# Half-width first pass for four token blocks instead of two in an attention and two-MLP kernel

## The chip, the cores and the metric

One core of a Trainium2 chip runs the whole program in one launch. The metric is the device time of one execution in microseconds (us). Below, TensorE is PE, its weight loads PEld, VectorE DVE, ScalarE ACT, GpSimd POOL, and SP the engine that only issues transfers.

## The reference

Banded attention with 32 global tokens (batch 4, 8 heads, 544 positions, head dimension 64), then a squared-ReLU MLP, then a gated linear MLP. All arrays are fp32.

```
s_g = scale * q_g @ k_all.T ;           out_g = softmax(s_g) @ v_all
s_l = concat(scale * q_l @ k_g.T, banded(scale * q_l @ k_l.T))
out_l = softmax(s_l) @ v_all
x = concat(out_g, out_l) as (2176 tokens, 512)
x = (relu(x @ w_in) ** 2) @ w_out        # first MLP: 512 -> 2048 -> 512
y = ((x @ w1) * (x @ w2)) @ w3 @ w_out2  # second MLP
```

## The kernel before, in words

**Precision.** Every fp32 factor of a large product is split into a high and a low part, and a product is three matmuls (`PASSES`, line 66): high times high, high times low, low times high. So each weight has to be brought to that form first. `conv(n)` (line 527) does it for one piece of 128x512: two ACT instructions (lines 441, 444), two DVE instructions (452, 457), one POOL addition (523 or 513), and a split on ACT (465) and DVE (466).

**Blocks and halves.** The 2176 tokens are 8 blocks of 256 or 288 tokens, two to a batch. The first MLP is cut in two halves of its 2048 hidden columns. In its first half a block needs 16 converted pieces: 8 of `w_in` (0 to 7) and 8 of `w_out` (8 to 15). `h_unit` (line 579) computes 128 hidden columns of a block with 12 matmuls, then ReLU and square on ACT and the split of the result; `x_chain` (line 601) sums 128 of the 512 output columns over the hidden ones. Its result, a partial sum, goes to DRAM (`part_d`) and is added to the second half's later.

**Few blocks.** The first blocks come before all 16 pieces are converted. `width(i)` (line 81) says how many of a block's 8 hidden units are passed the first time: `HEAD` = 4 for the blocks below `FEW` = 2, 8 for the others. What the first two blocks leave out is done behind block 7, by `rows` (line 625) with the pieces 4 to 7 and 12 to 15, and `end_few` (line 724) adds it to the partial sum that `load_x` (line 715) has read back.

**Order.** The outer loop (line 730) goes over pairs of blocks. In the pair i the MLP of blocks i and i+1 is the main list of steps; the attention of the next batch (`cycle`, line 377: scores `sc` and `sg`, softmax on DVE and ACT, transposes `tp` and `tg`, the product `o` with the values) is laid between its steps by `merge` (line 643), and so are the conversions, the pieces 8 to 15 within the first pair. The first block of a pair needs the attention that was laid between the pair before: the copies of `o` to `xb` on ACT, their cast `hl` (line 571) and their split on DVE. From block 6 on there is no attention left. Behind the blocks' rest follow the first MLP's second half and the second MLP.

What stands in the program's text is not yet the order of an engine: the framework orders every engine's instructions anew, by readiness and a planned time, except where `keep_in_program_order` ties two. Each engine then works strictly in that order. The PSUM tiles `sc`, `tp`, `tg` and `o` share four banks (tag `at`).

Of the kernel before, what the change touches and what calls it, by code (L numbers as in the profile page):

```python
# [60 lines left out]
def block(i):  # L61
    i %= NBLK
    return S * (i // 2) + HALF * (i % 2), HALF if i % 2 == 0 else S - HALF
# [9 lines left out]

HEAD, FEW = 4, 2
ORDERED = (0, 1, 2, 3, 8, 9, 10, 11, 4, 5, 6, 7, 12, 13, 14, 15)
BREAKS = (*RUNS, 2 * HEAD)

# [1 line left out]
def width(i):  # L81
    return HEAD if i < FEW else 8
# [33 lines left out]
def attention_mlp(ctx: ExitStack, tc: tile.TileContext, kq0, kq, vw, wts, mask, ident, out_d):  # L116
# [321 lines left out]
    def conv_a(n):  # L438
        raw = raw_t.pop(n)
        t = [pools["cv"].tile([128, 512], I32, tag=f"wt{k}", name="wt", bufs=2) for k in range(3)]  # L440
        first = nc.scalar.activation(t[0].bitcast(F32), raw[:, :, 1].bitcast(F32), AF.Copy, scale=2.0**-112)
        if n >= 2 * HEAD:
            tc.keep_in_program_order(first)
        nc.scalar.activation(t[2], raw[:, :, 0].bitcast(U32), AF.Copy, scale=2.0**-29)
        mid_t[n] = t
        ahead = n + (4 if n < RUNS[1] else 3)
        if ahead < RUNS[1] or RUNS[1] <= n and ahead < RUNS[2]:
            load_w(ahead)

    def conv_b(n):  # L450
        a, b, _ = mid_t[n]
        first = nc.vector.tensor_scalar(
            out=b, in0=a, scalar1=3, scalar2=0x7FFFFFF8, op0=ALU.logical_shift_left, op1=ALU.bitwise_and
        )
        if n >= 2 * HEAD:
            tc.keep_in_program_order(first)
        nc.vector.scalar_tensor_tensor(  # L457
            out=b, in0=a, scalar=-(1 << 31), in1=b, op0=ALU.bitwise_and, op1=ALU.bitwise_or
        )
# [43 lines left out]
    def conv_c(n):  # L503
        _, b, m = mid_t.pop(n)
        if n >= PAIRED:
            k, u = divmod(n - PAIRED, 2)
            if u == 0:
                both_t[k] = unit("u1", F32)
                if "s" in both_t:
                    o, x, s = both_t.pop("s")  # L510
                    nc.sync.dma_start(out=both_d[o], in_=x)
                    nc.sync.dma_start(out=sums_d[o], in_=s)
            nc.gpsimd.tensor_tensor(out=both_t[k][:, u].bitcast(I32), in0=b, in1=m, op=ALU.add)  # L513
            if u == 1:
                x = both_t.pop(k)
                s = add_up(x, "u1", nc.vector)
                if k < 4:
                    both_t["s"] = k, x, s
                else:
                    for f in split_blocks(FIRST[k - 4], k, x, s, "u1"):  # L520
                        f()
            return
        nc.gpsimd.tensor_tensor(out=b, in0=b, in1=m, op=ALU.add)  # L523
        t = w_t[ORDERED[n] if n < RUNS[1] else n] = unit(UNITS[n])
        split_w(t, slice(0, 512), b.bitcast(F32))

    def conv(n):

        if n in BREAKS:
            conv_a(n)  # L530
        else:
            conv_c(n - 1)
        conv_b(n)
        if n + 1 in BREAKS:
            conv_c(n)
        else:
            conv_a(n + 1)
# [22 lines left out]
    def x_parts(i, k, n):  # L560

        t = xb_t[i, k] = fixed[4 * (i % 2) + k] if fixed else parts(NB)
        return t[:, :, :n]

    def of_split(i, k):
        s, n = block(i)
        return xs_d[:, k, :, s : s + n]
# [7 lines left out]
    def load_split(i, k, turn=1):  # L575
        t = xh[NBLK * turn + i, k] = x_parts(i, k, block(i)[1])
        nc.sync.dma_start(out=t.bitcast(F32), in_=of_split(i, k))

    def h_unit(i, f, w):
        n = block(i)[1]  # L580
        h = ps.tile([128, 512], F32, tag="h", name="h", bufs=H_BUFS)[:, :n]
        w = w_t[w]
        chain(h, [(w[:, a, 128 * k : 128 * (k + 1)], xh[i, k][:, b]) for k in range(4) for a, b in PASSES])
        r = sb.tile([128, NB], F32, tag="tmp", name="r", bufs=4)[:, :n]
        g = g_t[f] = fixed[8 + f % 6][:, :, :n] if fixed else parts(n)
        nc.scalar.activation(r, h, AF.Relu)  # L586
        nc.scalar.activation(g[:, 0], r, AF.Square)  # L587
        if i < SHARED:
            nc.vector.tensor_tensor(out=r, in0=r, in1=r, op=ALU.mult)
        else:  # L590
            nc.scalar.activation(r, r, AF.Square)  # L591
        split_lo(nc.vector, g[:, 1], r, g[:, 0])
# [3 lines left out]
    def staged(i, d):  # L596
        if d == 0:
            st_t[0] = sb.tile([128, 4, NB], F32, tag="st", name="st", bufs=1)[:, :, : block(i)[1]]
        return st_t[0][:, d, :]
# [25 lines left out]
    def rows(i, w_in, w_out, split, end, at=0):  # L625

        n, m = block(i)[1], len(w_in)
        steps = []
        for f in range(m + 1):
            if f < m:  # L630
                steps.append(lambda f=f: (h_unit(i, f, w_in[f]), store_now() if f == 1 else None))
            if at <= f < at + 4:
                steps.append(lambda f=f: split(f - at))
            if f > 0:
                steps.append(lambda f=f: x_add(i, f - 1, w_t[w_out[f - 1]], n, f == m))
        steps.append(lambda: [end(d) for d in range(4)])
        return steps

    def of(t, i):
        s, n = block(i)  # L640
        return t[:, :, s : s + n]
# [53 lines left out]
    main = [lambda f=f: h_unit(0, f, f) for f in range(width(0))]  # L695
# [9 lines left out]
    def split_a(i, d):  # L705
        if i < NBLK:
            split_x(i, d, xcols(i)[:, d])
        else:
            load_split(0, d, 2)
# [5 lines left out]
    def load_x(i):  # L715

        if i < NBLK:
            if "x" not in extra:
                extra["x"] = sb.tile([128, 4, 2 * NB], F32, tag="xb", name="xl", bufs=2)
            at = NB * (i % 2)  # L720
            t = x_t[i] = extra["x"][..., at : at + block(i)[1]]
            nc.sync.dma_start(out=t, in_=of(part_d, i))

    def end_few(i, d):
        nc.vector.tensor_tensor(out=staged(i, d), in0=acc[d], in1=x_t[i][:, d], op=ALU.add)
        if d == 3:
            nc.sync.dma_start(out=of(part_d, i), in_=st_t[0])
            load_x(i)

    for i in range(0, NBLK, 2):  # L730
        main = []
        for j in (i, i + 1):
            if j >= SHARED:
                if j == SHARED:
                    main.append(fix_places)
                main += rows(
                    j, range(8), range(8, 16),
                    lambda d, j=j: split_a(j + 1, d), lambda d, j=j: end_a(j, d, acc[d]),
                )
                continue  # L740
            if j > 0:
                main += [lambda f=f, j=j: h_unit(j, f, f) for f in range(width(j))]
            main += [lambda d=d, j=j: x_unit_a(j, d) for d in range(4)]
        b = i // 2 + 1
        if b < B:
            if b == 1:
                load_kq(H // 2)
                for k in range(H, H + 4):
                    load_v(k)
            steps = [s for j in range(4 * b - 1, 4 * b + 4) for s in cycle(j, j < 4 * b + 3, j >= 4 * b)]  # L750
            fills = [(steps, 0, len(main) - 5)]
            if b == 1:
                fills.append(([lambda n=n: conv(n) for n in range(2 * HEAD, 16)], 0, len(main)))
        else:
            for cm in (at_cm, rot_cm, cv_cm):
                cm.__exit__(None, None, None)
            pools["u2"] = ctx.enter_context(pool("u2", "right"))
            cv_cm = pool("cv2")
            pools["cv"] = cv_cm.__enter__()
            extra["w"] = sb.tile([128, 8 * NB], F32, tag="xb", name="wx", bufs=2)  # L760
            for k in range(16, 19):
                load_w(k)
            main.insert(18, lambda: (load_x(0), load_x(1)))
            for j in range(FEW):
                main += rows(
                    2 * NBLK + j, range(HEAD, 8), range(8 + HEAD, 16),
                    (lambda d: load_split(1, d, 2)) if j == 0 else lambda d: load_split(0, d),
                    lambda d, j=j: end_few(j, d),
                )
            fills = [([lambda n=n: conv(n) for n in range(16, 30)], 0, len(main))]  # L770
        merge(main, *fills)
# [187 lines left out]
    main = []  # L959
    for i in range(NBLK):  # L960
# [3 lines left out]
            lambda d, i=i: end_b(i, d), 0 if i < NBLK - 1 else 4,  # L964
# [102 lines left out]
    main = []  # L1067
# [140 lines left out]
```

## Time and profile before

| what | value |
| --- | --- |
| median of 3 runs | 861.88 us (860.67 to 863.28) |
| the profiled execution | 860.88 us, its span 859.1 us |
| busy: PE, PEld | 826.6 us (96%), 789.1 us (92%) |
| busy: DVE, ACT, POOL | 588.9 us (69%), 493.6 us (57%), 222.2 us (26%) |
| mean granted PE clock over the span | 0.99 |

The span is what lies between the first and the last instruction; the time of an execution is 1.78 us more. A row of the timeline is one or more like instructions in a run: its start in us from the span's start, its duration, engine, line, operation, what it writes and reads, how many, and in brackets the idle time before it with what ended it. The matmuls of a run overlap each other; the distance between the starts of two runs is therefore the better price for the first of them. A row of the stretches gives for each engine the busy time and the instructions in it, then the granted PE clock as a share of full speed.

### The profile page before, as it was taken

What the parts mean: (1) busy time and instruction counts of PE and PEld (TensorE: products, weight loads), DVE (VectorE), ACT (ScalarE), POOL (GpSimd) and SP (SyncE); (2) the same over time, 40 slices, a digit from 0 to 9 for tenths busy, and PEclk for the clock granted to TensorE, in tenths of its full rate; (3) what the DMA queues carried; (4) which work ended last, traced back from release to release, by engine and by line L of the source; (5) the groups of instructions that cost most, each with busy time, mean ns of one, the idle gap of its engine ahead of it and who ended that gap; (6) DMA issues with size and microseconds to landing.
All of it is one profiled execution on the core that took longest, in us unless ns stands there. A gap on an engine that the chain in (4) does not pass through costs nothing. (4 is left out here: it accounts for less than half of the span.)

```text
span 859.1 us, 17937 instructions
## 1 busy us (share of the span) xinstructions
PE 826.6 (96%) x6664; PEld 789.1 (92%) x6664; DVE 588.9 (69%) x1617; ACT 493.6 (57%) x1325; POOL 222.2 (26%) x264
## 2 busy tenths in 40 slices
PE   5789889999999999999999999999999999989998
PEld 4568779999999999999999999999999999989998
DVE  7878979773856576676742027796885857689862
ACT  7767977663767787777763246777311211355650
POOL 3401322000200333233330003330287445442000
PEclk9899989999999999999999999999999999999999
DMA  9935442333050776775853239745347544839931
GB/s 330 276 126 160 150 128 64 108 108 123 27 178 26 255 252 204 267 234 172 255 165 120 68 119 329 250 159 173 126 157 251 164 143 137 288 127 323 337 142 53
DMA packets 89879, 151.96 MB, mean 177 GB/s; under 512 B 6336, under 2 KB 63296, under 8 KB 89792
## 3 DMA queue, kind: packets, MB, share of 16 engines
q1 hardware_dynamic: 89792, 150.82, 53.4%
q8 instruction: 52, 0.85, 0.4%
q14 instruction: 35, 0.29, 0.1%
HBM read 103.42 MB, written 47.38 MB: 176 GB/s over the span
## 5 line engine op out<-in xcount | busy, mean ns | idle before, releaser
L162 PE MATMUL h<-hl,u 128*128 128x256 f32 (+1 forms) x1536 | 229.4, 291 | 6.1 <-ACT hl L571 4.9
L162 PEld LDWEIGHTS h<-hl,u 128*128 128x128 f32 x1536 | 205.1, 188 | 12.3 <-ACT hl L571 5.8
L816 PE MATMUL m<-hl,u 128*128 128x272 f32 x1296 | 171.2, 288 | 2.8 <-DVE r L838 1.5
L816 PEld LDWEIGHTS m<-hl,u 128*128 128x128 f32 x1296 | 165.5, 188 | 3.4 <-DVE r L838 2.0
L620 PE MATMUL acc<-hl,u 128*128 128x256 f32 (+1 forms) x1056 | 153.2, 288 | 0.2 <-DVE hl L151 0.2
L620 PEld LDWEIGHTS acc<-hl,u 128*128 128x128 f32 x1056 | 141.1, 188 | 1.2 <-DVE hl L151 0.4
L151 DVE TENSOR_TENSOR hl<-r,hl 128x288 fp32r<-128x288 f32 (+1 forms) x128 | 75.8, 598 | 76.1 <-ACT r L591 75.2
L523 POOL TENSOR_TENSOR wt<-wt 128x512 int32<-128x512 int32 x56 | 73.8, 1318 | 205.6 <-DVE wt L457 130.8
L586 ACT ACTIVATE r<-h 128x288 f32<-128x288 f32 (+1 forms) x128 | 49.7, 393 | 70.6 <-PE h L162 70.0
L162 PE MATMUL x<-hl,u 128*128 128x256 f32 (+1 forms) x480 | 70.4, 294 | 0.6 <-ACT pg L294 0.6
L816 PE MATMUL m<-u,u 128*128 128x272 f32 x528 | 70.3, 286 | 0.4 <-DVE r L836 0.2
L237 ACT ACTIVATE p<-p,st 128x192 f32<-128x192 f32 (+1 forms) x128 | 58.9, 464 | 16.0 <-DVE st L233 15.9
L816 PEld LDWEIGHTS m<-u,u 128*128 128x128 f32 x528 | 67.2, 188 | 0.8 <-DVE r L836 0.4
L162 PEld LDWEIGHTS x<-hl,u 128*128 128x128 f32 x480 | 62.9, 188 | 3.3 <-ACT pg L294 1.4
L466 DVE TENSOR_TENSOR u<-wt,u 128x512 fp32r<-128x512 f32 x56 | 40.3, 720 | 35.3 <-ACT u L465 34.7
L833 ACT COPY r<-m 128x272 f32<-128x272 f32 x40 | 15.4, 384 | 75.2 <-PE m L816 70.3
L270 POOL CAST qgp<-kq_hl 64x32 fp32r<-64x32 f32 x48 | 22.7, 473 | 138.5 <-PE sg L162 102.9
L1010 POOL TENSOR_TENSOR rs<-rs 128x272 f32<-128x272 f32 x64 | 56.2, 888 | 3.4
L587 ACT ACTIVATE hl<-r 128x288 fp32r<-128x288 f32 (+1 forms) x128 | 54.4, 432 | 4.0 <-ACT r L586 1.2
L1009 POOL TENSOR_TENSOR rs<-rs 128x272 f32<-128x272 f32 x32 | 28.2, 880 | 103.2 <-DVE rs L846 103.2
L457 DVE SCALAR_TENSOR_TENSOR wt<-wt 128x512 int32<-128x512 int32 x72 | 49.5, 688 | 1.6
L513 POOL TENSOR_TENSOR u<-wt 128x512 int32<-128x512 int32 x16 | 22.5, 1411 | 102.9 <-DVE wt L457 81.9
(113 smaller groups left out, 1309.4 us busy)
## 6 DMA issues: line engine op xcount, KB each, us to landing
wraw<-in_wts SPq DMA_DIRECT2D x37, 512.0 KB, 4.4
q_d<-rs SPq DMA_DIRECT2D x16, 952.0 KB, 5.3
rl<-q_d SPq DMA_DIRECT2D x12, 1088.0 KB, 7.3
wx<-in_wts SPq DMA_DIRECT2D x19, 512.0 KB, 5.1
u<-in_wts SPq DMA_DIRECT2D x16, 512.0 KB, 6.3
v_f<-in_vw SPq DMA_DIRECT2D x24, 256.0 KB, 2.9
hl<-xs_d SPq DMA_DIRECT2D x20, 288.0 KB, 4.1
hl<-xs_d SPq DMA_DIRECT2D x20, 256.0 KB, 4.4
```

Source lines behind the costliest of these rows:

```text
L151: eng.tensor_tensor(out=lo, in0=raw, in1=hi.bitcast(F32), op=ALU.subtract)
L162: mm(o, w, x, start=(k == 0), stop=(k == len(terms) - 1))
L237: nc.scalar.activation(p[:, c], p[:, c], AF.Exp, bias=least[:, n : n + 1], scale=-1.0, accum_out=sums[:, n, 0:1],)
L457: nc.vector.scalar_tensor_tensor(out=b, in0=a, scalar=-(1 << 31), in1=b, op0=ALU.bitwise_and, op1=ALU.bitwise_or)
L466: s = nc.vector.tensor_tensor(out=t[:, 1, cols], in0=raw, in1=t[:, 0, cols].bitcast(F32), op=ALU.subtract)
L523: nc.gpsimd.tensor_tensor(out=b, in0=b, in1=m, op=ALU.add)
L586: nc.scalar.activation(r, h, AF.Relu)
L587: nc.scalar.activation(g[:, 0], r, AF.Square)
L620: mm(acc[d], w[:, a, 128 * d : 128 * (d + 1)], g_t[f][:, b], start=(f + k == 0), stop=(last and k == 2),)
L816: mm(o, w, x, start=(i in (1, 6, 5, 4) and k == 0), stop=(k == len(terms) - 1), skip_group_check=(i in (2, 7, 3)),)
L1009: nc.gpsimd.tensor_tensor(out=u.c12, in0=u.c12, in1=u.c22, op=ALU.mult)
L1010: sub = lambda o, a, c: nc.gpsimd.tensor_tensor(out=o, in0=a, in1=c, op=ALU.subtract)
```

## The change

`FEW` becomes 4: blocks 2 and 3, too, pass only 4 of 8 hidden units the first time, and their rest is made behind block 7 with that of blocks 0 and 1. The conversions of the pieces 8 to 11 stay with the first pair's list, those of 12 to 15 go to the second pair's. The loads of the split inputs and of the partial sums for the four rests go round by block.

```diff
-HEAD, FEW = 4, 2
+HEAD, FEW = 4, 4
...
     def end_few(i, d):
         if d == 3:
             nc.sync.dma_start(out=of(part_d, i), in_=st_t[0])
-            load_x(i)
+            load_x((i + 2) % FEW)
...
-            if b == 1:
-                fills.append(([lambda n=n: conv(n) for n in range(2 * HEAD, 16)], 0, len(main)))
+            if b < 3:
+                some = ((2 * HEAD, 12), (12, 16))[b - 1]
+                fills.append(([lambda n=n: conv(n) for n in range(*some)], 0, len(main)))
...
             for j in range(FEW):
                 main += rows(
                     2 * NBLK + j, range(HEAD, 8), range(8 + HEAD, 16),
-                    (lambda d: load_split(1, d, 2)) if j == 0 else lambda d: load_split(0, d),
+                    lambda d, j=j: load_split(j + 1, d, 2) if j + 1 < FEW else load_split(0, d),
                     lambda d, j=j: end_few(j, d),
                 )
```

How the engines' order answers to it is seen at two places. The first is DVE at the end of the first pair, where the last two of the 16 conversions stand (L452 and L457 are the conversion's first two instructions on DVE, L466 its last; `u_...` is the converted piece; L151 splits the first block of the second pair). A row with - is of before, with + of the change:

```order
 L452 TENSOR_SCALAR wt<-wt 128x512
 L457 SCALAR_TENSOR_TENSOR wt<-wt 128x512
 L354 COPY xb<-o 128x32
 L151 TENSOR_TENSOR hl<-xb,hl 128x256
-L466 TENSOR_TENSOR u_1795<-wt,u_1795 128x512
-L452 TENSOR_SCALAR wt<-wt 128x512
+L466 TENSOR_TENSOR u_2676<-wt,u_2676 128x512
 L288 TENSOR_REDUCE stg_91<-sg 64x1
+L452 TENSOR_SCALAR wt<-wt 128x512
 L356 TENSOR_TENSOR xb<-xb,o 128x32
 L288 TENSOR_REDUCE stg_91<-sg 64x1
```

The names differ, and one conversion instruction has moved behind one other row. All rows of DVE ahead of these are the same in both, the conversions among them.

The second place is PE in the second pair, where the last heads of the second batch get their scores (`sc`) and the softmax of the heads before is transposed (`tp`, from `p_...`); `h` and `x` are the MLP's matmuls. Before:

```order
L162 MATMUL h<-hl,u_1128 128x288 x3
L156 MATMUL sc<-kq_hl 128x192
L162 MATMUL h<-hl,u_1128 128x288 x3
L156 MATMUL sc<-kq_hl 128x192 x5
L156 MATMUL sc<-kq_hl 128x224 x6
L320 MATMUL tp<-ident_sb,p_82 128x128 x4
L320 MATMUL tp<-ident_sb,p_83 128x128 x4
L162 MATMUL h<-hl,u_1128 128x288 x6
L162 MATMUL h<-hl,u_1373 128x288 x12
L307 MATMUL tg<-ident_sb,pg 128x64 x5
L156 MATMUL sc<-kq_hl 128x224 x6
L156 MATMUL sc<-kq_hl 128x192 x6
```

The same place in the change:

```order
L162 MATMUL h<-hl,u_222 128x256
L162 MATMUL h<-hl,u_293 128x256
L320 MATMUL tp<-ident_sb,p_80 128x128 x4
L162 MATMUL h<-hl,u_222 128x256 x2
L162 MATMUL h<-hl,u_293 128x256 x2
L320 MATMUL tp<-ident_sb,p_81 128x128 x4
L156 MATMUL sc<-kq_hl 128x192 x6
L156 MATMUL sc<-kq_hl 128x224 x6
L320 MATMUL tp<-ident_sb,p_82 128x128 x4
L320 MATMUL tp<-ident_sb,p_83 128x128 x4
L307 MATMUL tg<-ident_sb,pg 128x64 x5
L156 MATMUL sc<-kq_hl 128x224 x6
```

Before, 18 `h` matmuls of block 3 stand between `tp` and `tg`, and 63 of its `x` matmuls follow behind the last `o` of the batch. In the change block 3's matmuls are used up ahead of these rows; the `h` matmuls left are the first unit's of block 4, which wait for this very attention.

## Rows read from the trace of the kernel before

**Rows 1.** The page, busy time of each engine: us, share, instructions.

```profile
PE 826.6 (96%) x6664; PEld 789.1 (92%) x6664; DVE 588.9 (69%) x1617; ACT 493.6 (57%) x1325; POOL 222.2 (26%) x264
```

**Rows 2.** Stretches: length, busy PE PEld DVE ACT POOL, PEclk, DMA share, GB/s.

```profile
88.00:107.00 19.00, 16.74 (x176) 14.58 (x173) 18.91 (x77) 18.14 (x60) 6.84 (x10) 1.00 0.51 157
...
115.00:131.00 16.00, 12.29 (x110) 10.17 (x107) 11.95 (x38) 11.51 (x33) 2.79 (x2) 0.79 0.40 123
...
140.00:500.00 360.00, 360.00 (x2914) 343.49 (x2913) 214.75 (x604) 234.62 (x612) 67.14 (x65) 1.00 0.49 156
...
340.00:370.00 30.00, 30.00 (x244) 30.00 (x243) 22.02 (x42) 24.15 (x56) 7.80 (x6) 1.00 0.77 259
```

**Rows 3.** Timeline of PE, the end of the first pair and the second's start.

```profile
100.95 2.30 PE L156 MATMUL o<-pt_f,v_f 128*64 128x160 f32 x36
...
113.13 0.77 PE L162 MATMUL x<-hl,u 128*128 128x288 f32 x4
113.74 0.64 PE L162 MATMUL h<-hl,u 128*128 128x256 f32 x4
114.31 0.34 PE L307 MATMUL tg<-ident_sb,pg 64*128 64x64 f32 x2
...
115.47 2.60 PE L156 MATMUL o<-pt_f,v_f 128*64 128x160 f32 x36
118.89 1.09 PE L320 MATMUL tp<-ident_sb,p 128*128 128x128 f32 x8 [0.82 <-DVE p L245]
121.46 1.21 PE L162 MATMUL h<-hl,u 128*128 128x256 f32 x6 [1.48 <-ACT hl L571]
123.99 1.94 PE L320 MATMUL tp<-ident_sb,p 128*128 128x128 f32 x8 [1.32 <-DVE p L245]
125.86 4.25 PE L156 MATMUL o<-pt_f,v_f 128*64 128x160 f32 x36
130.04 1.02 PE L162 MATMUL sg<-kq_hl,qgp 128*128 128x288 f32 x6
...
131.27 0.97 PE L162 MATMUL h<-hl,u 128*128 128x256 f32 x6
```

**Rows 4.** Timeline of DVE between the same rows.

```profile
116.03 0.38 DVE L233 CUSTOM_DVE_ANT_0 p<-sc,mask_sb 128x224 f32<-128x224 f32 x1
...
117.92 0.68 DVE L466 TENSOR_TENSOR u<-wt,u 128x512 fp32r<-128x512 f32 x1
118.53 0.56 DVE L245 TENSOR_SCALAR p<-p,st 128x192 f32<-128x192 f32 x2
119.00 0.42 DVE L452 TENSOR_SCALAR wt<-wt 128x512 int32<-128x512 int32 x1
119.34 1.32 DVE L151 TENSOR_TENSOR kq_hl<-kqraw,kq_hl 128x1120 fp32r<-128x1120 f32 x1
...
120.64 0.68 DVE L457 SCALAR_TENSOR_TENSOR wt<-wt 128x512 int32<-128x512 int32 x1
121.24 0.18 DVE L354 COPY xb<-o 128x32 f32<-128x32 f32 x1
...
123.77 0.68 DVE L466 TENSOR_TENSOR u<-wt,u 128x512 fp32r<-128x512 f32 x1
```

**Rows 5.** Timeline of PE, dense runs at full clock.

```profile
283.11 6.54 PE L162 MATMUL x<-hl,u 128*128 128x288 f32 x48
289.49 4.76 PE L162 MATMUL h<-hl,u 128*128 128x256 f32 x39
...
369.31 4.42 PE L620 MATMUL acc<-hl,u 128*128 128x256 f32 x36
373.56 1.46 PE L162 MATMUL h<-hl,u 128*128 128x256 f32 x11
```

**Rows 6.** One line's instructions: L725, xcount, ns min/median/max, first and last start.

```profile
L725 DVE TENSOR_TENSOR st<-acc,xl x8: 415/437/454, 348.8 to 366.2; 128x256 f32<-128x256 f32 x4, 128x288 f32<-128x288 f32 x4
```

**Rows 7.** The page, DMA issues: xcount, KB each, us to landing.

```profile
hl<-xs_d SPq DMA_DIRECT2D x20, 288.0 KB, 4.1
```

## The prediction

> **What bounds the kernel now.** I read the page first: PE is busy for 826.6 of the 859.1 us [rows 1], so the time can only move by what PE waits, by its clock, or by work added to it. Then the stretches, to find where PE waits. From 140 to 500 us, in which the second and third pair, the four-unit rests and the second half lie, PE is busy all the time at full clock [rows 2]. Near the first pair it is not: 88 to 107 leaves it idle 19.00 - 16.74 = 2.3 us with DVE busy 18.91 of 19.00, and 115 to 131 idle 16.00 - 12.29 = 3.7 us with the granted clock at 0.79 [rows 2], which is a loss of 0.21 x 16 = 3.4 us more. So about 9.4 us are lost around the first pair. Last the timelines of PE and DVE in the second of these stretches, for what PE waits for [rows 3, 4]: the last attention of the batch runs there with next to no MLP matmuls left beside it, and PE waits for the softmax (L245) twice and for the split of the next block's input (L571) once [rows 3].
>
> That stretch is the model for the whole forecast, so I take it apart. From the start of `o` at 115.47 to the `h` run at 131.27 are 15.8 us [rows 3]. The path in it: scores are ready at 115.47; DVE takes them up at 116.03 and hands the last softmax over at 123.77 [rows 4]; PE transposes (123.99), multiplies with the values (125.86), makes the next `sg` (130.04), and the `h` run can go on [rows 3]. In the 7.74 us on DVE conversions have 0.61 (117.92 to 118.53) + 0.34 (119.00 to 119.34) + 0.60 (120.64 to 121.24) = 1.55 us [rows 4]. The clock: at 123.99 the same eight transposes take 1.94 instead of 1.09 us, and the same 36 `o` 4.25 instead of 2.30 us [rows 3], the lower of PE's two levels, 1.2 instead of 2.4 GHz, which costs 0.85 + 1.95 = 2.8 us. What is left is 15.8 - 1.55 - 2.8 = 11.4 us, the path at full clock and without conversions. PE's own work in it is two `o` of 2.30, 16 transposes and six `h` (1.09 + 1.09 + 0.75), and `sg` with 1.0: 8.5 us. So the bare path keeps PE waiting 2.9 us; conversions and the clock make it dear.
>
> **The change part by part.**
>
> *The conversions.* The text moves four of them to the second pair. The order of DVE doesn't: up to the split of block 2 all rows are the same, conversions included, and the one that shows a difference has moved behind a single row. So nothing is taken from the 88 to 131 us in which DVE is full: 0 us. Bounds: nothing, and the four conversions' whole DVE time, dealt with as a rival.
>
> *The matmuls that move.* Blocks 2 and 3 leave out four hidden units each: 4 x 12 matmuls of `h` and, for the four groups of output columns, 4 x 12 of `x`, 96 for a block. A run of 48 with 288 columns takes 289.49 - 283.11 = 6.38 us, 0.133 each; a run of 36 with 256 columns 373.56 - 369.31 = 4.25 us, 0.118 each [rows 5]. That is 96 x 0.118 + 96 x 0.133 = 24.1 us out of the second pair and the same 24.1 us behind block 7, since the rest's runs (`acc`) have the price of the others [rows 5]: 0 us, if PE is as full here as there.
>
> *What the rests add.* Eight more additions on DVE (L725), 0.437 us each [rows 6], 3.5 us; two more stores and loads of partial sums; eight more loads of split input, of 4.1 us for 288 KB [rows 7], issued by SP a block's 12 us ahead. All lie beside 24 us of PE work in a stretch like 340 to 370, where the two rests of before stand: PE full, DVE busy 22.0 of 30.0 [rows 2], so 8 us of DVE in 30 are free. 0 us; the upper bound, were every addition to hold PE up once a block for its length, is 8 x 0.44 = 3.5 us, and nothing here can gain. The conversions of the second half's weights run beside more PE work than before, where PE waited for nothing anyway: 0 us.
>
> *The second pair without its filler.* This is the term that counts. Before, block 3 still has 63 `x` matmuls when the second batch's last `o` is done: the attention is finished long before block 4 needs it. In the change block 3's matmuls are used up before the last heads' scores. From there on the order of PE reads as in the first pair's end, and one step longer: in the first pair an `x` and an `h` run of four stand before `tg` (113.13 to 114.31 [rows 3]), here nothing does. `tg` needs one of the four banks that the scores before hold until DVE has read them, so those 1.2 us become a wait. Then comes the path taken apart above: conversions are over by then (none of this second pair's on DVE), so 11.4 us with 8.5 us of work: 2.9 us. Sum at full clock: 4.1 us. The clock: in the first pair it fell after waits of 0.82, 1.48 and 1.32 us [rows 3]; in the second the waits are of the same kind and somewhat more in sum, so I take that it falls here too and hits the same transposes and `o`: 2.8 us. Sum 6.9 us. Bounds: below, no wait (0 us, if the order's reach into block 4 and the third batch fills it); a gain is excluded, since PE was full here before. Above, the path as dear as in the first pair (15.8 - 8.5 = 7.3 us) with 1.2 us before it and a second fall of the clock of 2.8 us: 11.3 us.
>
> *The third pair* has blocks of full width and the order of before: 0 us.
>
> The Trainium skill has a rule against this change: Perfetto Trace Analysis, Optimization Strategy (under Identifying Performance Opportunities), says that where regimes with different busiest engines alternate, interleaving them may help; the change unweaves attention and MLP. By it the second pair would become like the first, which lost 9.4 us; by the path it loses 6.9 us. The first is kept as a rival (dearer).
>
> **Sum.** The profiled execution took 860.88 us, 859.1 of them its span; the median of the runs shown is 861.88, 1.0 higher. 860.9 + 6.9 = 867.8 from the execution, 868.8 from the median. I say 868.5 us, nearer the median.
>
> **The rivals.**
>
> *The clock holds.* The waits stay as worked out, but no fall comes with them: 861.9 + 4.1 = 866.0, or 865.0 from the profiled execution; 865.5. For it: conversions no longer stretch the waits, of which the longest would be under those of the first pair. Against it: the fall of the first pair came with no wait longer than 1.48 us [rows 3]. Beside this stands the Trainium skill, TensorE: Matmul & The Clock Gate, HAM oscillation, which lays the fall to a wait for data between bursts that is long against the burst; by it the short waits here would leave the clock up. The trace disagrees as far as it goes: three short ones sufficed.
>
> *No new wait.* PE's order reaches far enough, the third batch's scores and block 4's first units come up in time, and the moved work is paid back one to one: 862. For it: PE was full for 360 us [rows 2] and DVE will have only attention to do. Against it: what is left to fill with waits for this very attention.
>
> *The first pair is relieved after all (faster).* If the four conversions' work leaves 88 to 131 us, DVE there has less by four times 0.61 + 0.34 + 0.60, with the waits that hang on it: 6.2 us, of the 9.4 us lost there. It decides from the point where the first pair saves more than the second's 4.1 us, which it does only if nearly all of it is on the path. With the clock up in both: 861.9 - 9.4 + 4.1 = 856.6, say 857. For it: DVE is full in 88 to 107 [rows 2]. Against it: the order of DVE, in which they stand where they stood. That the change doesn't do what it says is thus for the conversions the likely case, and part of the forecast.
>
> *Dearer.* The second pair loses as much as the first, 861.9 + 9.4 = 871.3, or the upper bound, 861.9 + 11.3 = 873.2: DVE and ACT also late for the heads before the last, or a second fall of the clock. For it: the waits begin a step earlier than in the first pair. Against it: no conversions are among them. I put it at 873.
>
> **How the numbers follow.** Chances: forecast 0.60; the clock holds 0.18; no new wait 0.13; first pair relieved 0.05; dearer 0.04. What a measurement can tell from no change is 0.3%, 2.6 us: from 859.3 to 864.5. The forecast and the dearer case are slower, the clock's rival for 0.12 of its 0.18: 0.76. Same: 0.13 less 0.01, and 0.06: 0.18. Faster: 0.05 + 0.01 = 0.06. The range from 863 to 873 leaves out most of no new wait, the relieved first pair and half of the dearer case, together 0.19.
>
> **What would show it.** In the profile after, PE's row of the first 131 us is that of before, with conversions on DVE at the same times and the same two stretches of loss. Then, some 24 us before the end of what was the second pair, waits of PE for L245, L571 and the reading of scores, each 1 to 3 us, 4 us in sum, with the granted clock at 0.5 for some us beside them. Behind block 7 four rests instead of two, with PE full. It is wrong if the conversions thin out before 131 us, if the second pair's end shows no waits, or if the rests behind block 7 do: then the moved work itself has a price.

## The result, and the profile after

The changed kernel takes 867.44 us (median of four runs, 866.11 to 868.90) where the kernel before, run beside it, takes 862.20 us (four runs). The ratio on record is 1.0070, 95% interval 1.0047 to 1.0093, which is 4.1 to 8.0 us; the two medians alone stand at 1.0061, 5.2 us. It is slower; forecast were 868.5 us, range 863 to 873. The profiled execution took 866.11 us, its span 863.8, to be set against 860.88 and 859.1 before.

The page of the changed kernel first, busy time of each engine. Read it for what it can't tell: PE has the same 6664 matmuls and still shows 4.4 us more busy time than in [rows 1], while its idle time is the same within 0.3 us (32.5 before, 32.8 after). The loss doesn't show there as idleness; it has to be read by stretches.

```profile
PE 831.0 (96%) x6664; PEld 791.5 (92%) x6664; DVE 587.7 (68%) x1617; ACT 497.2 (58%) x1333; POOL 217.9 (25%) x264
```

The stretches of the changed kernel, with the columns of [rows 2]: the first two are the first pair, the next two the end of the second, the last one the rests.

```profile
88.00:107.00 19.00, 17.21 (x174) 15.15 (x174) 18.91 (x73) 18.16 (x60) 6.94 (x10) 1.00 0.53 164
115.00:131.00 16.00, 12.06 (x100) 9.82 (x96) 12.25 (x39) 10.68 (x29) 4.15 (x5) 0.79 0.48 149
160.00:180.00 20.00, 19.32 (x187) 17.00 (x187) 13.33 (x62) 14.87 (x51) 0.83 (x4) 1.00 0.44 138
180.00:200.00 20.00, 18.22 (x168) 16.04 (x165) 13.50 (x62) 11.93 (x42) 0.83 (x4) 0.91 0.34 109
340.00:370.00 30.00, 30.00 (x235) 29.66 (x234) 22.98 (x43) 21.95 (x50) 9.07 (x7) 1.00 0.85 291
```

The first pair is where it was: DVE full from 88 to 107, PE idle 3.9 us from 115 to 131, clock 0.79. (DVE is full only up to 107, not up to 131 as the prediction has it: from 115 to 131 it is busy for 12.0 us of 16 before and 12.3 here.) New is 160 to 200: PE waits 0.68 + 1.78 = 2.46 us there and the clock falls to half for 3.4 us (the 0.91 over 20 us; before, PE was full at full clock from 140 to 500 [rows 2]). Where the four rests stand, PE is as full as it was.

Now the timeline of PE at the second pair's end, to be laid beside [rows 3]: start, length, operation, and in brackets the wait before it and who ended it.

```profile
174.98 0.35 PE L156 MATMUL sc<-kq_hl 64*128 64x192 f32 x1
175.73 0.92 PE L156 MATMUL sc<-kq_hl 64*128 64x192 f32 x11 [0.39 <-ACT pt_f L325]
176.58 1.09 PE L320 MATMUL tp<-ident_sb,p 128*128 128x128 f32 x8
177.91 0.52 PE L307 MATMUL tg<-ident_sb,pg 64*128 64x64 f32 x5 [0.24 <-ACT pt_f L322]
178.48 1.22 PE L156 MATMUL sc<-kq_hl 64*128 64x224 f32 x12
179.63 2.30 PE L156 MATMUL o<-pt_f,v_f 128*64 128x160 f32 x36
182.23 0.68 PE L320 MATMUL tp<-ident_sb,p 128*128 128x128 f32 x4 [0.30 <-DVE p L245]
183.06 0.50 PE L162 MATMUL h<-hl,u 128*128 128x256 f32 x2 [0.15 <-ACT hl L571]
184.39 0.74 PE L162 MATMUL h<-hl,u 128*128 128x256 f32 x4 [0.82 <-DVE hl L151]
184.97 0.60 PE L320 MATMUL tp<-ident_sb,p 128*128 128x128 f32 x4
186.07 1.81 PE L320 MATMUL tp<-ident_sb,p 128*128 128x128 f32 x8 [0.50 <-DVE p L245]
187.81 3.17 PE L156 MATMUL o<-pt_f,v_f 128*64 128x160 f32 x36
190.91 1.02 PE L162 MATMUL sg<-kq_hl,qgp 128*128 128x288 f32 x6
...
192.15 0.97 PE L162 MATMUL h<-hl,u 128*128 128x256 f32 x6
```

It is the first pair's pattern: `o`, a wait for the softmax (L245), six `h` behind the cast and the split of the next block's input (L571 on ACT, L151 on DVE), another wait for L245, `o`, `sg`. The waits are shorter than in the first pair, and the last transposes and `o` run slow (1.81 for 1.09, 3.17 for 2.30). Not one matmul of an MLP stands between `sc` at 174.98 and the two `h` at 183.06: the filler is used up.

In the first pair of the changed kernel the timeline of PE reads as in [rows 3], with the same three waits.

```profile
113.03 0.34 PE L307 MATMUL tg<-ident_sb,pg 64*128 64x64 f32 x2
...
114.19 2.60 PE L156 MATMUL o<-pt_f,v_f 128*64 128x160 f32 x36
117.61 1.09 PE L320 MATMUL tp<-ident_sb,p 128*128 128x128 f32 x8 [0.82 <-DVE p L245]
120.18 1.21 PE L162 MATMUL h<-hl,u 128*128 128x256 f32 x6 [1.47 <-ACT hl L571]
122.71 1.94 PE L320 MATMUL tp<-ident_sb,p 128*128 128x128 f32 x8 [1.33 <-DVE p L245]
124.58 4.04 PE L156 MATMUL o<-pt_f,v_f 128*64 128x160 f32 x36
128.55 1.02 PE L162 MATMUL sg<-kq_hl,qgp 128*128 128x288 f32 x6
```

The timeline of DVE beside it answers to [rows 4]: the conversions (L452, L457) still lie among the softmax and the splits.

```profile
117.24 0.56 DVE L245 TENSOR_SCALAR p<-p,st 128x192 f32<-128x192 f32 x2
117.72 0.42 DVE L452 TENSOR_SCALAR wt<-wt 128x512 int32<-128x512 int32 x1
118.05 1.32 DVE L151 TENSOR_TENSOR kq_hl<-kqraw,kq_hl 128x1120 fp32r<-128x1120 f32 x1
...
119.36 0.68 DVE L457 SCALAR_TENSOR_TENSOR wt<-wt 128x512 int32<-128x512 int32 x1
```

### The profile page after: what moved, and what is told of

Its sections match the earlier page's. It is cut to its first block, busy times and chain, and to the rows that moved or that the text cites. A ratio compares the mean times of both kernels' runs of the same rounds, so it can differ in the third digit from the quotient of the medians.

```text
span 863.8 us, 17966 instructions
## 1 busy us (share of the span) xinstructions
PE 831.0 (96%) x6664; PEld 791.5 (92%) x6664; DVE 587.7 (68%) x1617; ACT 497.2 (58%) x1333; POOL 217.9 (25%) x264
## 5 line engine op out<-in xcount | busy, mean ns | idle before, releaser
L162 PE MATMUL h<-hl,u 128*128 128x288 f32 (+1 forms) x1536 | 229.5, 291 | 6.0 <-ACT hl L571 4.3
L620 PE MATMUL acc<-hl,u 128*128 128x288 f32 (+1 forms) x1152 | 167.6, 288 | 0.2 <-DVE hl L151 0.2
L620 PEld LDWEIGHTS acc<-hl,u 128*128 128x128 f32 x1152 | 154.2, 188 | 1.4 <-DVE hl L151 0.4
L151 DVE TENSOR_TENSOR hl<-r,hl 128x288 fp32r<-128x288 f32 (+1 forms) x128 | 72.9, 576 | 90.5 <-ACT r L591 89.7
L523 POOL TENSOR_TENSOR wt<-wt 128x512 int32<-128x512 int32 x56 | 74.1, 1324 | 230.3 <-DVE wt L457 118.8
L237 ACT ACTIVATE p<-p,st 128x224 f32<-128x224 f32 (+1 forms) x128 | 59.1, 465 | 12.9 <-DVE st L233 12.7
L466 DVE TENSOR_TENSOR u<-wt,u 128x512 fp32r<-128x512 f32 x56 | 40.3, 720 | 36.2 <-ACT u L465 35.2
L162 PE MATMUL x<-hl,u 128*128 128x256 f32 (+1 forms) x384 | 58.0, 295 | 0.6 <-ACT pg L294 0.6
L162 PEld LDWEIGHTS x<-hl,u 128*128 128x128 f32 x384 | 50.6, 188 | 3.2 <-ACT pg L294 1.4
L270 POOL CAST qgp<-kq_hl 64x32 fp32r<-64x32 f32 x48 | 19.8, 412 | 123.2 <-PE sg L162 74.4
L457 DVE SCALAR_TENSOR_TENSOR wt<-wt 128x512 int32<-128x512 int32 x72 | 49.5, 688 | 1.6
L320 PE MATMUL tp<-ident_sb,p 128*128 128x128 f32 x256 | 40.8, 303 | 8.5 <-DVE p L245 8.2
```

Of the source, the lines that this page charges most:

```text
L151: eng.tensor_tensor(out=lo, in0=raw, in1=hi.bitcast(F32), op=ALU.subtract)
L162: mm(o, w, x, start=(k == 0), stop=(k == len(terms) - 1))
L237: nc.scalar.activation(p[:, c], p[:, c], AF.Exp, bias=least[:, n : n + 1], scale=-1.0, accum_out=sums[:, n, 0:1],)
L320: nc.tensor.transpose(tp[:, k, :], p[:, at : at + 128], ident_sb)
L457: nc.vector.scalar_tensor_tensor(out=b, in0=a, scalar=-(1 << 31), in1=b, op0=ALU.bitwise_and, op1=ALU.bitwise_or)
L466: s = nc.vector.tensor_tensor(out=t[:, 1, cols], in0=raw, in1=t[:, 0, cols].bitcast(F32), op=ALU.subtract)
```

## The experiments

**My theory**: the loss is the second pair's end, whose filler went to the rests; moving the conversions in the text changes nothing, since the emitted order keeps them at the first pair. **The rivals**: each rest costs something of its own; or the conversions did move and hurt; or any MLP work will do as filler, not block 3's at the end alone. Runs 1, 2, 4 and 5 were timed against 861.28 us of before (30 runs), runs 3, 6 and 7 against 861.51 us (23 runs). The diffs of runs 2, 3, 5 and 6 are against the kernel before, the others against the change; lines that only keep loads and buffers in step are left out, marked `...`.

**1. The change with the conversions listed as before.**

```diff
-            if b < 3:
-                some = ((2 * HEAD, 12), (12, 16))[b - 1]
-                fills.append(([lambda n=n: conv(n) for n in range(*some)], 0, len(main)))
+            if b == 1:
+                fills.append(([lambda n=n: conv(n) for n in range(2 * HEAD, 16)], 0, len(main)))
```

> Four blocks at half width as in the change, but all conversions listed with the first pair as before: one part of the change undone. Theory (the loss is the missing filler at the end of the second pair; the listing of the conversions changes no order): the time of the change, 866.5 to 868.5 us. Rival (the split of the conversions over two pairs is what cost): back toward the time before, 862 to 864 us.

Measured: 867.72 us, ratio 1.0069 (1.0045 to 1.0093), against 1.0070 for the whole change. That half of the change does nothing that can be told; the loss belongs to the widths. The profile of this run also shows the second pair's end without a fall of the clock. PE's order and waits are those of the changed kernel, but the last transposes and `o` run at full speed:

```profile
190.21 1.06 PE L320 MATMUL tp<-ident_sb,p 128*128 128x128 f32 x8 [0.49 <-DVE p L245]
191.20 2.30 PE L156 MATMUL o<-pt_f,v_f 128*64 128x160 f32 x36
```

**2. Block 3 whole again.** Blocks 0 to 2 pass half, the loads and buffers follow, the conversions are listed as before.

```diff
-HEAD, FEW = 4, 2
+HEAD, FEW = 4, 3
...
```

> Blocks 0, 1 and 2 at half width, block 3 at full width, conversions as before; the places of the reloaded inputs shifted by one so that three rests alternate. Theory (what matters is block 3's filler beside the last heads of the second batch): no waits at the second pair's end, 861.5 to 863.5 us. Rival (every rest costs the same, by its reload, its additions or its place): half of the change's loss, 864 to 866 us.

Measured: 862.48 us, ratio 1.0008 (0.9991 to 1.0025). One rest more than before and no loss that can be told (the interval leaves room for at most 2.2 us), so no price of a rest by itself shows. Its stretch at the second pair's end, columns as above:

```profile
160.00:200.00 40.00, 40.00 (x376) 36.52 (x374) 24.02 (x101) 24.51 (x78) 1.88 (x5) 1.00 0.35 101
```

**3. Block 2 whole instead of block 3.** Blocks 0, 1 and 3 pass half.

```diff
-HEAD, FEW = 4, 2
+HEAD, FEW = 4, 3
+SOME = (0, 1, 3)
...
-    return HEAD if i < FEW else 8
+    return HEAD if i in SOME else 8
...
```

> Blocks 0, 1 and 3 pass half of the sum, block 2 all of it; the conversions are listed with the first pair as before. It asks whether the run with block 3 whole lost nothing because block 3's work stands at the end of the second pair, or because any one whole block is enough filler. Theory (the end needs filler): the second half of block 2's products is taken up before the last softmax and transposes, so part of the loss comes back: 864 to 867, with waits of the tensor engine in the second pair's last 10 us. Rival (any 12 us of filler will do): 861.5 to 863, as with block 3 whole, and the tensor engine busy throughout from 160 to 200 us.

Measured: 863.20 us, ratio 1.0012 (0.9996 to 1.0029). The time lies below my theory's range and 0.2 us above the rival's; PE's rows decide for the rival: it need not be block 3. PE is full from 160 to 200 with block 2's `x` reaching to the last softmax (line numbers are one higher here):

```profile
186.51 1.09 PE L321 MATMUL tp<-ident_sb,p 128*128 128x128 f32 x8
187.36 2.89 PE L163 MATMUL x<-hl,u 128*128 128x288 f32 x20
190.09 1.34 PE L163 MATMUL h<-hl,u 128*128 128x256 f32 x10
```

The transposes at 186.51 follow `o` without a wait here, and 20 `x` and 10 `h` stand behind them, where the changed kernel has six `h` and waits. So 12 us of the 24 us suffice, from either block; only the last 12 us taken away cost time that can be told.

**4. The change with its conversions truly held back.** In the changed kernel the scheduler leaves conversions 12 to 15 at the first pair. Here GpSimd first copies one element of the first batch's last output into each conversion's buffer, so that they can't start before. A conversion's first half is otherwise done with the second half of the one ahead; the entry 12 in `BREAKS` parts them there.

```diff
-BREAKS = (*RUNS, 2 * HEAD)
+BREAKS = (*RUNS, 2 * HEAD, 12)
...
+        if 12 <= n < 16:
+            nc.gpsimd.tensor_copy(t[0].bitcast(F32)[:, :1], xcols(2)[:, 3, :1])
```

> The change, with the conversions of pieces 12 to 15 really held back until the first batch's attention is done (one element of its last result is copied by GpSimd into the conversion's buffer first). Theory: the first pair's path loses the 1.55 us of conversions on VectorE, and perhaps part of the clock's fall, the second pair's waits stay: 864 to 866.5 us. Rival (the first pair is bound by VectorE as a whole, so four conversions less give 6 us): 860 to 862 us. If they collide with the second pair's attention instead: 867 us or more.

Measured: 862.15 us, ratio 1.0007 (0.9991 to 1.0024): 5.3 us less than the change, more than my theory gave, and 0.15 us above the rival's range. The rival's reason isn't what the trace shows: from 88 to 107 DVE is as full as it was (18.91 us of 19) and PE waits 1.9 us (1.8 in the changed kernel). What is gained lies at the first pair's end:

```profile
114.75 0.34 PE L307 MATMUL tg<-ident_sb,pg 64*128 64x64 f32 x2
...
115.91 2.30 PE L156 MATMUL o<-pt_f,v_f 128*64 128x160 f32 x36
118.52 1.09 PE L320 MATMUL tp<-ident_sb,p 128*128 128x128 f32 x8 [0.31 <-DVE p L245]
...
120.62 0.74 PE L162 MATMUL h<-hl,u 128*128 128x256 f32 x4 [0.77 <-DVE hl L151]
121.28 1.24 PE L320 MATMUL tp<-ident_sb,p 128*128 128x128 f32 x8
122.45 2.30 PE L156 MATMUL o<-pt_f,v_f 128*64 128x160 f32 x36
124.68 1.02 PE L162 MATMUL sg<-kq_hl,qgp 128*128 128x288 f32 x6
```

From `tg` to `sg` are 9.93 us; in the changed kernel 15.52, of which the clock has 2.6 (the 12.90 of run 3, which had no fall there, see below). The second pair pays part of it back, as waits without a fall of the clock: 1.68 + 1.44 + 2.02 = 5.1 us from 140 to 200, where the changed kernel had 2.5 us and the clock.

```profile
140.00:160.00 20.00, 18.32 (x169) 16.39 (x169) 18.04 (x61) 14.84 (x45) 8.55 (x10) 1.00 0.33 100
160.00:180.00 20.00, 18.56 (x196) 15.96 (x193) 16.46 (x80) 16.27 (x59) 2.76 (x5) 1.00 0.40 124
180.00:200.00 20.00, 17.98 (x170) 16.50 (x170) 13.90 (x60) 12.28 (x44) 1.34 (x6) 1.00 0.37 109
```

**5. The kernel before, with the same conversions held back** and listed with the second pair's first eight steps of rows.

```diff
-BREAKS = (*RUNS, 2 * HEAD)
+BREAKS = (*RUNS, 2 * HEAD, 12)
...
+        if 12 <= n < 16:
+            nc.gpsimd.tensor_copy(t[0].bitcast(F32)[:, :1], xcols(2)[:, 3, :1])
...
-            if b == 1:
-                fills.append(([lambda n=n: conv(n) for n in range(2 * HEAD, 16)], 0, len(main)))
+            if b < 3:
+                some, upto = (((2 * HEAD, 12), len(main)), ((12, 16), 8))[b - 1]
+                fills.append(([lambda n=n: conv(n) for n in range(*some)], 0, upto))
```

> The kernel before (two blocks at half width) with the same four conversions really held back until the first batch's attention is done; block 2 needs them for its output matmuls soon after. Theory: 1.5 to 3.5 us off the first pair's path and no loss in the second, where PE was full: 859 to 861 us. Rival: block 2's output matmuls now wait for the late pieces, 862 us or more.

Measured: 860.15 us, ratio 0.9984 (0.9961 to 1.0007): within the theory's range, but no gain that can be told from none, and not as the theory has it. The first pair is relieved as in run 4 (`tg` to `sg` 9.93 us, which is more than the theory gave), and the second, where no loss was expected, pays it back: PE waits 2.0 us from 140 to 160, and a wait of 1.27 us comes with 6.8 us at half clock. Blocks 2 and 3 are whole here and need all weights early, and conversions (L468, L454, L459) stand on DVE shortly ahead of the L299 that PE waits for. That they alone made the wait isn't shown, since DVE is no fuller from 140 to 160 than before (18.66 us, before 18.84). The two waits:

```profile
147.89 0.53 PE L162 MATMUL h<-hl,u 128*128 128x288 f32 x2 [0.64 <-ACT hl L573]
149.69 0.45 PE L307 MATMUL tg<-ident_sb,pg 64*128 64x64 f32 x2 [1.27 <-DVE pg L299]
```

**6. Only block 0 half.** Block 1 is whole, its `x` is to fill the first pair's end, and its weights are converted within 12 steps.

```diff
-HEAD, FEW = 4, 2
+HEAD, FEW = 4, 1
...
-                fills.append(([lambda n=n: conv(n) for n in range(2 * HEAD, 16)], 0, len(main)))
+                fills.append(([lambda n=n: conv(n) for n in range(2 * HEAD, 16)], 0, 12))
...
```

> Only block 0 passes half; block 1 is whole, so its products are there as filler for the first pair's end, and its weights are converted within the first pair's first 12 steps of rows. Theory (a pair's end waits for lack of filler): the tensor engine's waits of 0.82, 1.48 and 1.32 us at the first pair's end and the 3.4 us that the low clock costs there shrink: 857 to 861. Rival (the first pair's end is held up by the conversions themselves, which still run on VectorE and ScalarE there, and block 1's products wait for them): no gain, 862 to 866.

Measured: 862.34 us, ratio 1.0012 (0.9994 to 1.0030); no gain. Its three long waits are gone (the longest at the first pair's end is 0.46 us), but PE now waits earlier, 1.4 us between 107 and 115, while DVE and ACT are full:

```profile
107.00:115.00 8.00, 6.63 (x74) 5.89 (x73) 7.92 (x34) 7.97 (x28) 3.34 (x5) 1.00 0.25 75
```

The time and this stretch are on the rival's side: the first of the waits (0.70 us) is for a conversion's split on ACT. But the first pair's end did get better (PE idle 1.0 us from 115 to 131 at full clock), so part of what kept the time from falling isn't accounted for.

**7. Three half blocks and the conversions held back**: run 2's widths with run 4's delay.

```diff
-HEAD, FEW = 4, 4
+HEAD, FEW = 4, 3
...
-BREAKS = (*RUNS, 2 * HEAD)
+BREAKS = (*RUNS, 2 * HEAD, 12)
...
+        if 12 <= n < 16:
+            nc.gpsimd.tensor_copy(t[0].bitcast(F32)[:, :1], xcols(2)[:, 3, :1])
...
```

> Blocks 0 to 2 pass half, block 3 all of it, and the four last conversions of the first half are held back until the first batch's attention is through (a copy of one element into the conversion's buffer makes them wait). Theory (two separate effects: the first pair's end is held up by conversions on VectorE and ScalarE, the second pair's end by the lack of filler): from the 862.5 us of the same widths without the delay, 5.6 us go at the first pair's end (15.5 us from the transposes of the tiled weights to the next softmax's sums in the changed kernel, 9.9 in the run with delayed conversions), and some 3 us come as waits between 140 and 180 us, as in that run: 859 to 861. Rival (the delay only moves the wait to the second pair, as it did in the run of the kernel before with delayed conversions, where the clock fell anew): 861.5 to 864.

Measured: 856.23 us (855.36 to 858.63), ratio 0.9942 (0.9922 to 0.9962). This beats both kernels: 5.3 us under the one before, 6.3 us under the same widths without the delay, more than I expected. The waits that I took over from run 4 don't come. Block 3 is there to fill and only block 3 needs the late weights; that this is the reason fits runs 4 and 5, where one of the two is missing:

```profile
115.00:131.00 16.00, 14.92 (x162) 13.12 (x161) 10.71 (x52) 12.66 (x43) 1.13 (x6) 1.00 0.58 172
140.00:200.00 60.00, 59.73 (x560) 55.02 (x559) 48.33 (x183) 42.48 (x135) 11.43 (x22) 1.00 0.37 111
```

## Why the prediction was right, and where its sizes were off

**The conversions (0 us): right.** Order and trace agree, and run 1 shows it by itself: with or without the listing the time is the same within the noise. What would have come of a real move is run 4.

**The moved matmuls (24.1 us out and back): right.** By line and shape PE has 48 fewer `x` of each width and 48 more `acc` of each, at the same mean. The group of one width in the changed kernel (line, operation, count | busy us, mean ns):

```profile
L620 PE MATMUL acc<-hl,u 128*128 128x256 f32 x576 | 78.9, 281 | 0.2 <-DVE hl L151 0.2
```

and of the kernel before:

```profile
L620 PE MATMUL acc<-hl,u 128*128 128x256 f32 x528 | 72.3, 281 | 0.2 <-DVE hl L151 0.2
```

Summed from each start to the next on PE, `acc` gains 12.1 us and `x` loses 12.1; the `h` that moved stay `h`.

**The rests (0 us): right**, by PE's full 30 us from 340 to 370 and by run 2.

**The second pair without its filler (6.9 us): right in mechanism and sum, off in its parts.** Summed in the same way from the first `h` run behind the first pair (131.27 before, 129.78 after) to PE's last matmul (ends at 855.49 and 860.74), PE takes 6.7 us more, and nearly all of it lies at the attention's own operations: transposes 2.9, scores and tiled weights 1.6, `o` 1.2. The parts:
- Waits, forecast 4.1 us. Shown as idle are 0.39 + 0.24 + 0.30 + 0.15 + 0.82 + 0.50 = 2.4 us. On top comes what a run loses at its end when nothing follows at once: eight transposes take 1.09 us, but behind the same eight at full flow the next run starts 0.85 us after their start. Four such ends before a wait (after `tp`, `tp`, `h`, `tp`) make about 1.0 us, an estimate from these two numbers. Together 3.4 us. No wait is as long as the 1 to 3 us that the prediction named as its sign.
- Clock, forecast 2.8 us. It fell for 3.4 us instead of 6.8, and hit the last eight transposes (1.81 - 1.09) and `o` (3.17 - 2.30): 1.6 us. This is the term that was mis-sized, and run 1 shows that it isn't a fixed one: with the same order and waits and no fall there, PE takes 5.2 us more than before over the same stretch. So the fall is 1.6 us, and the rest, forecast 4.1, is 5.2.
- Some 1.7 us of the 6.7 I can't put to a single wait.

That 6.9 and 6.7 lie so close is luck: the waits were put too low and the clock too high.

The time rose by 5.2 us and not by 6.7 because the changed kernel's profiled run reaches that `h` run 1.5 us earlier, though PE's order up to there is the same. A fall of the clock at 54.8 us, which of the two only the run of before has, is as large: the transposes and scores there take 3.43 us (54.72 to 58.15) before and 1.87 us (54.97 to 56.84) in the changed kernel. The profiled runs of all seven experiments have a fall between 54 and 57 us, so it is the changed kernel's profiled run, the fastest of its four, that lacks it.

**A wrong step that cost nothing: the bare path.** I took the first pair's 15.8 us apart into 1.55 of conversions, 2.8 of clock and 11.4 of path. The runs give the three apart. From `tg` to `sg` before takes 130.04 - 114.31 = 15.73 us [rows 3]; in run 3, with the conversions in place but by chance no fall of the clock, 12.90; in runs 4, 5 and 7, without the conversions, 9.93, 9.93 and 9.94. So the clock is 2.83 (as forecast), the conversions 2.97, not 1.55. Counting only the conversions' time on DVE left out their work on two other engines. Before, ACT makes three conversion steps, 1.71 us, ahead of the last exponentials and the cast, and none in run 4; and while POOL makes a conversion's addition (L523), one of the softmax's four L245 lasts 1.16 us, its neighbours 0.31 to 0.32. Rows of before:

```profile
116.10 0.62 ACT L465 CAST u<-wt 128x512 fp32r<-128x512 f32 x1
116.62 0.68 ACT L441 ACTIVATE wt<-u 128x512 f32<-128x512 f32 x1
117.21 0.69 ACT L444 ACTIVATE wt<-u 128x512 int32<-128x512 uint32 x1
...
121.49 1.52 POOL L523 TENSOR_TENSOR wt<-wt 128x512 int32<-128x512 int32 x1 [7.32 <-DVE st L241]
121.97 1.88 DVE L245 TENSOR_SCALAR p<-p,st 128x192 f32<-128x192 f32 x4
```

In run 4, with no addition there, no L245 of the same stretch lasts over 0.33 us. How the 2.97 us part among the three engines isn't settled. Run 4 waits 0.31 and 0.77 us where the change waits 0.82, 1.47 and 1.33. From the start of `o` to the `h` run the clean path is 10.0 us (run 4, 115.91 to 125.91), not the prediction's 11.4, which still held part of the conversions' cost. In the second pair it is longer, 12.5 - 1.6 = 10.9 us, which brought the sum back to the forecast; why it is 0.9 us longer there isn't settled.

**The rivals.** "The clock holds" was nearly as close as the forecast: half of a fall came, and in run 1's profile none, so which of the two comes is a matter of the run. "First pair relieved" was rightly refused for the change as it is, and its mechanism is real: it is what runs 4 and 7 do. That run 7 reached its price (857 us) is luck, since the sum is another one: DVE from 88 to 107 stays full, the gain lies at the pair's end, and the filler is kept. "Dearer" didn't come: no single wait in the second pair is over 0.82 us.

The Trainium skill, Perfetto Trace Analysis, Optimization Strategy, says that regimes with different busiest engines may gain by interleaving. The runs agree and add a limit: with 12 of the 24 us that the change takes away left beside the second batch's attention there is no loss that can be told (ratio 1.0008), with none of them the ratio is 1.0070.

## What to carry to other kernels

Filler that can stand anywhere is worth the waits that it covers, and no more: before moving some, count how much of it is spare (here 12 of the 24 us moved were), and keep the rest for the end of the chain that it hides. Moving a helper in the source is not moving it on the engine; read the emitted order, and if a scheduler keeps it early, give it a dependency. A helper that runs beside a latency chain is to be counted on every engine that the chain passes, not on one alone (here 2.97 us, where DVE's share was 1.55), and is better put where a chain is covered.

## What the runs showed of the hardware

**The clock.** Its falls are not told by the waits alone. At the first pair's end the same three waits, 0.82, 1.48 and 1.32 us to within 0.02, came with 6.8 us at half clock before, after and in run 1, with 3.4 us in run 2, and with none in run 3. In run 4 a wait of 1.26 us and one of 0.76 stood close together at 180 to 184 with no fall, in the changed kernel 0.82 and 0.50 came with 3.4 us, in run 1 0.82 and 0.49 at the same place with none, in run 5 a wait of 1.27 us came with 6.8. The stretch of run 3:

```profile
115.00:131.00 16.00, 12.06 (x128) 10.12 (x126) 13.89 (x45) 12.61 (x37) 5.26 (x7) 1.00 0.57 170
```

In these 16 us PE makes 128 matmuls, in the changed kernel 100, at a granted clock of 1.00 instead of 0.79. So such a place cost 0, 1.4 or 2.8 us (12.90, 14.29 and 15.73 us from `tg` to `sg`), seen on one profiled execution each of five kernels (15.52 in the changed kernel); the prediction's remark that three short waits sufficed holds for four of the five. Among the 30 runs of the kernel before that runs 1, 2, 4 and 5 were timed against, the time goes with the clock: the five with a mean granted clock of 0.994 and more took 858.3 to 859.9 us, the five with 0.987 and less 862.4 to 865.3 us. A term for the clock is better given as these three values than as one.

**DVE beside POOL.** In the kernel before, six of the 128 L245 last over 0.5 us (median 0.32, longest 1.35), and each of the six overlaps an L523 on POOL; in the changed kernel it is six of six as well.
